# Linear attention and an MLP mixer on one core: the last rows of all eight batches as a ninth batch, part of the normalisation on ScalarE, and a new order of instructions

## The chip, the cores and the metric

One core of a Trainium2 chip runs the whole program. Five engines work side by side, each on its own queue of instructions in program order: TensorE (PE: matrix products into PSUM, eight banks of 128 partitions by 512 fp32 numbers), VectorE (DVE) and ScalarE (ACT), which read PSUM and write SBUF, GpSimd (POOL), and SyncE (SP), which here only issues transfers. An instruction that waits for another engine holds up everything behind it on its own queue. Transfers run on 16 DMA engines. The metric is device time in microseconds (us) of one execution, fp32 in and out, bf16 inside; smaller is better.

## The reference

```python
batch, n_heads, seq, head_dim = (8, 8, 576, 64)     # q, k, v
d_tok, d_ch = (256, 1536)                           # mixer, d_model = 512

def phi(x):
    return np.where(x > 0, x, np.exp(x) - 1.0) + 1.0
q_p, k_p = (phi(q), phi(k))
kv = np.einsum('bhsd,bhse->bhde', k_p, v)
z = np.sum(k_p, axis=2)
num = np.einsum('bhsd,bhde->bhse', q_p, kv)
den = np.einsum('bhsd,bhd->bhs', q_p, z)[..., None] + 1e-06
x = (num / den), heads side by side: (8, 576, 512)

xt = x.transpose(0, 2, 1)
h = np.maximum(xt @ w_tok1, 0.0) @ w_tok2           # along the 576 rows
u = x + h.transpose(0, 2, 1)
h2 = np.maximum(u @ w_ch1, 0.0) @ w_ch2             # along the 512 channels
return (u + h2)
```

The eight batches do not depend on one another. The channel step (`u @ w_ch1`, relu, `@ w_ch2`) works on each row by itself, so rows of several batches can be put together there.

## The kernel before, in words

**Tiling.** The 576 rows of a batch are 64 times 9. Two neighbouring row indices make a tile of 128 partitions: four such row tiles (R = 4, index r) and 64 rows that are left over, the last rows. A batch n goes through these stages:

- loads of q, k, v (`load`, L225, SP's queue), phi of k and q (`phi_exp` on ScalarE, `phi_add` and `phi_end` on VectorE, L250 to L262), the products of k and v (`kv`, L296), a copy to `kvbd` on ScalarE;
- q transposed by transfers on SP (`qtr_dma`, names `nqT0`, `nqT1`, L333), then numerator and denominator (`nd_mm`, name `nn`, 40 products into six banks);
- the division: for batches 2 to 7 `nd_den` and `nd_last` (L395, L404: the sum with eps and the reciprocal, two each, on VectorE) and five multiplications on VectorE, `nd_six` (three times) and `nd_one` (twice);
- the row step (`mm1` L443, `mm2` L454), u = x + h on VectorE (L470), u transposed by transfers on SP (`utr_dma`, L486);
- the channel step. Batches 0 and 1 use plain products there (`mm3` L683, batch 0 also `mm4` L742). From batch 2 on the first product, and from batch 1 on the second, are block products after Strassen and Winograd: seven products of half-size blocks in place of eight, bought with sums and differences of blocks (`u_sums` `nsK`, `row_sums` `nwK`, on VectorE). First product: `mix_mm` (names `nxGI`, group G of three, product I of seven, L913 to L931), read by `mix_read` (`nyGI`: I = 1, 4, 5, 6 on ScalarE, 2, 3, 7 on VectorE). Second product: `product` (`npIJ`, L960 to L972), for batches 1 to 6 read by `pair_copy` (ScalarE), `pair_end` (`neZ` and so on, VectorE) and `pair_more` (`nhZ`, POOL), written out by `pair_put` (`no`, POOL's queue).

**The last rows.** Two batches' last rows fill one tile of 128 rows, `ut`. The pairs (0, 1) and (2, 3) go through the channel step by plain products: `mm3_tail` (names `T00` to `T12`, L706) and `mm4` with t = 8 (`U00` to `U12`). The pairs (4, 5) and (6, 7) come together at the end: `mm3_tails` (`7c0` to `7c5`, L728), then block products (`tail_product`, L1017) with sums on POOL (`tail_sums`), while batch 7 is read in quarters (`product_read`, `product_put`) and its results leave on the queues of SP and ScalarE.

**Order.** `tc.manual_schedule()` is on: the list `ORDER` names every step behind the first batch's start, and each engine executes its own instructions in the order of that list; waits between engines follow from the data. `BANK`, `SLOT`, `EBUF` place each step's PSUM bank and buffer. `A0` to `A43` is the first batch up to its channel step, which the list keeps in the same order in both kernels.

Of the kernel before, what the change touches and what calls it, by code (L numbers as in the profile page):

```python
# [39 lines left out]
WHOLE = {'00', '01', 't0', 't1'}  # L40

BANK = {k_: int(v_) for k_, v_ in (e.split(":") for e in """2K:0 2n0:0 2n1:2 2n2:4 2f:6 2g0:3 2g1:6 2X2:5 2Z2:2 2Y2:1 2gt:6 3K:6 3n0:2 3n1:4 3n2:6 3f:3 3g0:6 3g1:6 3X2:2
3Z2:0 3Y2:5 3gt:4 4K:2 4n0:2 4n1:4 4n2:6 4f:6 4g0:4 4g1:0 4X2:2 4Z2:1 4Y2:3 4gt:6 5K:6 5n0:1 5n1:3 5n2:5 5f:5
5g0:5 5g1:3 5X2:4 5Z2:5 5Y2:7 5gt:1 6K:2 6n0:1 6n1:3 6n2:5 6f:2 6g0:5 6g1:2 6X2:4 6Z2:0 6Y2:6 6gt:6 7K:2 7n0:2
7n1:4 7n2:6 7f:2 7g0:0 7g1:2 7X2:3 7Z2:6 7Y2:1 7gt:5 2m2:0 2m3:1 2m4:2 2m5:3 2m8:1 2m9:1 2m10:0 2m11:1 3m2:0
3m3:1 3m4:2 3m5:3 3m8:1 3m9:0 3m10:0 3m11:1 4m2:0 4m3:1 4m4:2 4m5:3 4m8:1 4m9:1 4m10:0 4m11:1 5m2:0 5m3:1
5m4:2 5m5:3 5m8:1 5m9:0 5m10:0 5m11:1 6m2:0 6m3:1 6m4:2 6m5:3 6m8:1 6m9:1 6m10:0 6m11:1 1h00:7 1h01:6 1h10:5
1h11:6 1t0:7 1t1:0 1t2:1 1t3:6 1m0:2 1m1:0 1m2:0 1m3:4 1m4:5 1m5:6 1m6:6 1m7:2 1m8:5 1m9:7 1m10:1 1m11:6 T00:7
T10:3 T01:3 T11:0 T02:3 T12:7 U08:0 U18:3 7c0:3 7c1:4 7c2:4 7c3:6 7c4:2 7c5:4 7X0:5 7Z0:4 7Y0:1 7X1:2 7Z1:0
7Y1:0 7PX0:7 7PZ0:3 7PY0:1 7PX1:6 7PZ1:5 7PY1:5 7tX:0 7tZ:4 7tY:2 1PX:1 1PZ:2 1PY:5 2PX:0 2PZ:5 2PY:1 3PX:0  # L50
3PZ:3 3PY:4 4PX:7 4PZ:0 4PY:0 5PX:0 5PZ:7 5PY:1 6PX:7 6PZ:1 6PY:6 warm0:0 0Q00:1 0Q01:2 0s0:3 warm1:0 0Q10:1
0Q11:2 warm2:3 0K0:4 0d0:0 0n0:6 0l0:1 0s1:2 0K1:4 0d1:3 0n1:6 0l1:0 0f0:1 0f1:4 0g00:2 0g01:3 0g10:0 0t0:6
0t1:4 0g11:1 0m0:3 0m1:7 0t2:6 0t3:4 0m2:1 0m3:2 0gt:2 0m4:5 0m5:6 0m6:6 0m7:3 0m8:7 0m9:0 0m10:4 0m11:4 U00:1
U01:0 1Q0:4 U02:2 U03:3 1Q1:6 1K:4 1n00:6 1n01:6 1n10:4 1n11:4 1n20:4 1n21:6 1f:4 1g2:4 0ut:3 2X1:6 2Z1:4
2Y1:2 3X1:3 3Z1:5 3Y1:1 4X1:7 4Z1:0 4Y1:0 5X1:6 5Z1:0 5Y1:2 6X1:5 6Z1:6 6Y1:1 2X0:7 2Z0:3 2Y0:0 3X0:4 3Z0:0
3Y0:6 4X0:1 4Z0:7 4Y0:5 5X0:1 5Z0:5 5Y0:0 6X0:7 6Z0:3 6Y0:2""".split())}
# [1141 lines left out]
```

## Time and profile before

| | us |
|---|---|
| runs | 244.52, 245.35, 245.88; median 245.35 |
| span of the profiled execution, first to last instruction | 243.4 |
| PE busy, DVE busy, ACT busy, POOL busy in it | 233.1, 211.5, 136.4, 81.2 |
| end of the last product | 238.5 |
| last product to the end of the span | 4.9 |

The page of the profile shows one execution. Its own span is 243.4 us; what lies around it (start and end of the program) is not in the trace, and the median of the runs lies 1.95 us above it. Busy times are unions of the intervals of an engine's instructions; the shown duration of a matrix product reaches into the next one, so products are costed by the distance of their starts, which the chain of work gives.

### The profile page before, as it was taken

To read this page: it belongs to the slowest core of one execution; us is meant where nothing else is said; L and a number is where in the kernel's file an instruction comes from. 1 tells how busy PE (TensorE), PEld (TensorE's weight loads), DVE (VectorE), ACT (ScalarE), POOL (GpSimd) and SP (SyncE) were. 2 spreads that over 40 slices of the span, in tenths; PEclk is the share of its full clock that TensorE was granted. 3 is DMA by queue.
4 is the path that set the end of the run, shared out by engine and by line. 5 is a ranking of instruction groups with operands and counts; after the bars stand their busy time and mean duration, and the time that the engine had idled before them with its cause. 6 is when DMAs were issued, how large, how long until landed. Compare 5 with 4: busy or idle time off the path is not lost.

```text
span 243.4 us, 6361 instructions
## 1 busy us (share of the span) xinstructions
PE 233.1 (96%) x2597; PEld 174.2 (72%) x2616; DVE 211.5 (87%) x387; ACT 136.4 (56%) x224; POOL 81.2 (33%) x88
## 2 busy tenths in 40 slices
PE   7889989999999999999999999999999999999991
PEld 3575445464677686789867887688778867888881
DVE  5955786999999989999999999999999599867661
ACT  4773782669788277327994297448923542347000
POOL 8870044076910620035200520206015810440730
PEclk9999999999999999999999999999999999999999
DMA  6999989999979989978948989495782285143035
GB/s 230 278 202 260 317 260 234 409 283 286 365 225 198 270 265 161 247 97 305 285 127 175 370 262 200 82 260 178 161 138 40 44 171 112 24 91 81 3 80 180
DMA packets 49805, 48.42 MB, mean 199 GB/s; under 512 B 30064, under 2 KB 35568, under 8 KB 49776
## 3 DMA queue, kind: packets, MB, share of 16 engines
q1 hardware_dynamic: 41664, 35.00, 51.3%
q0 software_dynamic: 7472, 12.22, 25.5%
q10 hardware_dynamic: 640, 0.79, 1.0%
q8 instruction: 20, 0.33, 0.6%
q14 instruction: 9, 0.07, 0.1%
HBM read 35.85 MB, written 9.44 MB: 186 GB/s over the span
## 4 chain that ended last, share of the span: by engine, by line
PE 84%; DMA 9%; POOL 3%; issue 1%; DVE 1%; SPq 1%; POOLq 0%; DVEq 0%
PE ps L970 27%; PE ps L928 23%; PE ps L747 6%; PE ps L448 6%; DMA q_raw<-in_q_dram 5%; PE ps L459 4%; PE ps L686 4%; DMA wc<-in_moe_w_ch_dram 4%; PE ps L711 2%; PE ps L733 2%; PE ps L302 2%; PE ps L1024 2%; PE ps L387 2%; POOL qT L1111 1%; POOL cr L233 1%
## 5 line engine op out<-in xcount | busy, mean ns | idle before, releaser
L970 PE MATMUL ps<-k_raw,v_raw 128*128 128x256 bf16 x252 | 31.8, 273 | 0.0
L943 ACT COPY v_raw<-ps 128x512 f32<-128x512 f32 x30 | 17.0, 595 | 22.7 <-PE ps L928 21.5
L970 PEld LDWEIGHTS <-cr 128*128 128x128 bf16 x252 | 24.4, 98 | 4.8
L970 PEld LDWEIGHTS <-v_raw 128*128 128x128 bf16 x252 | 24.1, 98 | 3.8 <-issue 0.4
L928 PEld LDWEIGHTS <-swc 128*128 128x128 bf16 x240 | 23.4, 98 | 3.1
L681 DVE CUSTOM_DVE_ANT_0 cr<-ps,v_raw 128x512 bf16<-128x512 f32 x30 | 20.1, 684 | 4.5 <-PE ps L928 2.5
L928 PEld LDWEIGHTS <-wc 128*128 128x128 bf16 x216 | 21.1, 98 | 3.6
L928 PE MATMUL ps<-crt,swc 128*128 128x256 bf16 x180 | 23.1, 273 | 0.0
L252 ACT ACTIVATE e<-q_raw 128x1152 bf16<-128x1152 f32 x16 | 18.7, 1167 | 6.7 <-DMA q_raw<-in_q_dram 6.7
L686 PE MATMUL ps<-uT,wc 128*128 128x512 bf16 x91 | 21.6, 379 | 0.4 <-issue 0.2
L970 PE MATMUL ps<-wc,cr 128*128 128x256 bf16 x168 | 21.6, 273 | 0.0
L1071 POOL TENSOR_TENSOR obuf<-obuf,w 128x512 f32<-128x512 f32 x6 | 8.2, 1360 | 38.6 <-ACT w L1058 19.5
L252 ACT ACTIVATE e<-k_raw 128x1152 bf16<-128x1152 f32 x16 | 18.5, 1166 | 3.2 <-DMA k_raw<-in_k_dram 2.6
L1071 POOL TENSOR_TENSOR obuf<-obuf,q_raw 128x512 f32<-128x512 f32 x6 | 8.2, 1374 | 35.6 <-DVE obuf L1064 35.6
L928 PE MATMUL ps<-uT,wc 128*128 128x256 bf16 x144 | 19.5, 273 | 0.0
L1064 DVE TENSOR_TENSOR obuf<-ps,u 128x512 f32<-128x512 f32 x24 | 16.4, 685 | 2.5 <-PE ps L970 2.4
L1071 POOL TENSOR_TENSOR obuf<-obuf,part 128x512 f32<-128x512 f32 x6 | 7.7, 1289 | 26.5 <-DVE dens L400 18.5
L413 DVE TENSOR_TENSOR x<-ps,dens 128x768 bf16<-128x768 f32 x18 | 16.6, 930 | 0.0
L686 PEld LDWEIGHTS <-wc 128*128 128x128 bf16 x96 | 8.9, 98 | 10.0 <-issue 0.6
L470 DVE TENSOR_TENSOR u<-ps,x 128x1024 bf16<-128x1024 f32 x12 | 14.6, 1220 | 0.1
L836 DVE TENSOR_TENSOR v_raw<-cr 128x512 bf16<-128x512 bf16 (+3 forms) x24 | 14.5, 620 | 0.0
L448 PE MATMUL ps<-x,w 128*128 128x512 bf16 x50 | 13.9, 379 | 0.3
(168 smaller groups left out, 514.3 us busy)
## 6 DMA issues: line engine op xcount, KB each, us to landing
k_raw<-in_k_dram SPq DMA_DIRECT2D x16, 576.0 KB, 6.8
q_raw<-in_q_dram SPq DMA_DIRECT2D x16, 576.0 KB, 6.3
v_raw<-in_v_dram SPq DMA_DIRECT2D x14, 576.0 KB, 7.6
out_dram<-obuf POOLq DMA_DIRECT2D x12, 512.0 KB, 6.0
wc<-in_moe_w_ch_dram POOLq DMA_DIRECT2D x8, 384.0 KB, 9.3
out_dram<-obuf POOLq DMA_DIRECT2D x4, 256.0 KB, 7.3
cr<-in_v_dram POOLq DMA_DIRECT2D x2, 288.0 KB, 7.6
out_dram<-obuf POOLq DMA_DIRECT2D x4, 128.0 KB, 4.8
```

The lines of the kernel that those rows point to most:

```text
L252: nc.scalar.activation(out=ebuf[EBUF[f"{n}{nm}{c}"]], in_=f, func=AF.Exp)
L413: nc.vector.tensor_tensor(out=xv[:, :, rc0:rc0 + 3], in0=nd_tile(n, m)[:, :, k0:k0 + 6, 0:D].rearrange("p i (q a) d -> p i q a d", a=2), i ...
L448: nc.tensor.matmul(out=banks(f"{n}f")[:, mt], lhsT=w1t[:, b, ms] if r == R else w1[:, r, ms], rhs=x[b][:, r, :], start=(r == 0), stop=(r = ...
L470: nc.vector.tensor_tensor(out=u[b][:, rs], in0=banks(f"{n}g{i}"), in1=x[b][:, rs], op=ALU.add)
L681: nc.vector._custom_dve(TENSOR_ADD_SAT, out=o, in0=ps, in1=c, s0=3.4028234663852886e38, s1=0.0)
L686: nc.tensor.matmul(out=bank(f"{n}m{mc}"), lhsT=wc1[:, kj, 128 * mc:128 * mc + 128], rhs=uTj[b][:, kj] if n < 2 - U1 else uT[b][:, :, kj], ...
L747: nc.tensor.matmul(out=bank(f"U{p}{t}"), lhsT=crt[:, kc, :] if t == 8 else cr[b][:, kc, 128 * r:128 * r + 128], rhs=wc2[:, kc, :], start=( ...
L928: nc.tensor.matmul(out=ps[:, j], lhsT=lhs[:, k_, 128 * j:128 * (j + 1)], rhs=rhs[:, :, k_], start=(first and j == 0 and k_ == 0), stop=(k_ ...
L943: nc.scalar.copy(out={1: c1, 6: c6, 5: c5}[i], in_=ps)
L970: nc.tensor.matmul(out=ps, lhsT=lhs[:, k_], rhs=rhs[:, k_], start=(first and not skip and k_ == 0), stop=(k_ == KH - 1), skip_group_check= ...
L1064: nc.vector.tensor_tensor(out=slots(f"{n}P", 4)[:, d::2, HC[c]], in0=pair_tile(n, "X" if z == "W" else z), in1=u[n % 2][:, d::2, HC[c]], o ...
L1071: nc.gpsimd.tensor_tensor(out=o, in0=o, in1=part[i], op=ALU.add)
```

## The change

The last rows of all eight batches become a ninth batch (n = 8) with four row tiles, one for each pair of batches: `ut` is now 128 by 4 by 512, `uTt` holds its transpose, and `mix_mm`, `mix_read`, `row_sums`, `product` now run up to n = 8, and `product_read` for n = 8 alone. Batch 7 is treated like batches 1 to 6; batch 8 takes the place that batch 7 had, without its own table of weight sums. `mm3_tail`, `mm3_tails`, `tail_product` and what belongs to them are gone. The last rows of x have a tile of their own (`xt`), in which a batch writes only its 64 partitions, and the sum u of a pair is one instruction of 128 partitions (`mm2_tails_read`, `ngv`) in place of two of 64.

In the division, the sum with eps goes to ScalarE in three pieces (`nd`: names `nd0` to `nd2`), one reciprocal covers all 42 denominators (name `nnd`), the two multiplications of 128 elements become four scaled copies on ScalarE (`no0`, `no1`), and the third large one is split in two (`nn2`, `nnt`). `BANK`, `SLOT`, `EBUF` and the list `ORDER` behind `A43` are new as a whole; in the new list the two halves of a bank (`p10 p11`) follow one another.

```diff
-NO = 6
+NO = 4
...
-CUTS = {1: [0, 3, 6], 2: [0, 2, 6], 3: [0, 2, 6], 4: [0, 2, 6], 5: [0, 2, 6], 6: [0, 2, 6], 7: [0, 2, 4, 6]}
+CUTS = {1: [0, 3, 6], 2: [0, 2, 6], 3: [0, 2, 6], 4: [0, 2, 6], 5: [0, 2, 6], 6: [0, 2, 6], 7: [0, 2, 6], 8: [0, 2, 4, 6]}
...
-WHOLE = {'00', '01', 't0', 't1'}
+WHOLE = {'00', '01'}
...
-0mb1 0mb0 0ma6 0r0 0mb3 0r1 1ka0 0ma7 1kx0 0ma2 0ma8 0mb6 1kb0 0mb2 0r3 0mb8 0mb7 0r6 0r8 0ma4 0r7 G21 0gt
-1kx1 G22 0ma9 0gv 0ma10 0mb4 1ka1 0r2 0ma5 0r4 G11 0mb10 1kb1 0mb5 0r10 G23 0mb9 0r5 0ma11 0mb11 1qa0 1qx0 B0
-0r9 0q0 B1 0r11 1qb0 B2 1qx1 1qa1 1Q00 1Q01 0q1 1Qc01 1v0 1Qc00 0q2 1qb1 1v1 1Q10 1Q11 1K 1Qc11 2Lq0 ws02
-1Qc10 0q3 2Lq1 1Kc0 1Kc1 2Lv0 ws04 1n20 1n01 2Lk0 1nc20 0q4 2Lk1 1nc01 2Lv1 1n10 0q5 1nc10 1n00 0q6 1nc00 1n11
...
-6kx1 3p21 3w20 4uT1 5qb1 3p10 5Kc1 6kx0 3w22 3p11 5qT1 3eZ 3p50 3c0 6ka1 3p51 5Kc0 5qT0 3w40 U10 3c2 3w30 U11
-6Lq0 6Lq1 6kb1 U12 4s1 6ka0 3p31 V1 3p30 7Lk0 4s2 6Lv1 3p61 3eY 6Lv0 3p60 6kb0 7Lk1 5n 3c1 5nd 3hY 3p71 5ne
-3p70 5n0 3hZ 4x02 5o0 3eW 4x01 4x21 5n2 4y01 3hW 3p40 4y21 4y02 4x06 6qx0 5n1 4x05 4x26 4y06 6qa1 3p41 4y05
...
-7ta1 7R11 7R51 7p20 7w32 7t5 7R10 7ts2 7R50 7p61 7tb1 7p31 7R61 7ts4 7R20 7p30 7R31 7tr5 7p60 7tr1 7ts3 7p71
-7R60 7p21 7t6 7R21 7R30 7p70 7R71 7D200 7tr6 7t3 7D711 7D710 7ta2 7D201 7tr3 7D210 7R70 7tb2 7p41 7D311 7tr2
-7D310 7t7 7D211 7R41 7td20 7p40 7D411 7tr7 7D410 7t4 7td21 7R40 7D700 7D701 7tr4 7td70 7td71"""
...
+A31 A32 A35 A34 A36 A37 A38 1Lk0 A39 1Lk1 1Lv1 A40 1Lq0 A41 1Lq1 A42 1Lv0 A43 0ma0 At2 0ma1 At3 0ma3 0mb1 0ma5 G03
+0ma4 G01 1kx0 1ka0 1kb0 B0 G02 0ma7 0r1 G21 0mb4 0mb7 G22 0mb3 0r4 B1 0r3 0r7 0ma6 0mb6 1kx1 G11 0mb0 0r0 0mb5 G23
+0ma8 0ma2 0r6 1ka1 1kb1 0r5 0mb2 0r2 1v1 B2 2Lq0 2Lq1 0ma11 0mb11 0ma9 0mb9 G24 G13 G04 0r11 0ma10 0mb10 2Lv0 2Lk0 0r9
+1qx0 0r10 0q1 1qa0 1qb0 1qa1 1qx1 1qb1 0q0 1Q00 1Qc00 0mb8 0r8 1Q01 1Qc01 1v0 0q2 2Lk1 G12 1Q10 1K 1Qc10 G14 1Q11
+1Qc11 0q3 1Kc1 1Kc0 1n01 2qx0 2Lv1 1n00 wt0 ws04 ws14 1nc01 0q4 0q5 1n20 0q6 1nc00 1n21 0q7 1nc20 ws24 ws02 1nc21 1n10
...
+3y15 5v1 3y17 5K 5Kc0 3x04 5Kc1 3x13 3x24 3x14 3y04 4g1 3y14 6Lk1 5qb1 3p10 4gu0 3y13 3p11 5qT0 3y24 3p20 6qx0 3w10
+3w12 3p21 4gu1 3w22 3c0 3w20 3p50 3p51 3c2 3p61 3eZ 5qT1 5n 6kx1 3p60 6ka1 3w40 3p30 3w30 5d0 5d2 5d1 5nd 3p31 3c1 5o1
+6kb1 5n0 4uT0 5o0 3eY 3p71 6kx0 3p70 3eW 4x01 4x02 4uT1 4s1 5n2 3hZ 6qx1 4x12 5nt 3p40 7Lk1 3p41 4y01 4y02 4x11 4y11
+4x21 4y21 3eX 3hY 6Lv1 6v1 7Lv1 4s2 5n1 4x05 4x22 4y22 4x16 4x06 4y06 5f0 6qa1 7Lq1 3hW 3o 4y05 4s3 5f1 4x26 4x07 4y12
...
+8s3 7x24 8x15 8y16 8x21 8y06 8x05 7y24 7y17 7x14 8s4 8y21 8y05 8x07 7y14 8x26 8y07 8x17 8x03 7y22 7p10 7w20 7w12 8x02
+8y03 8x12 7p11 8y15 8y17 7c0 8y12 7p50 8y26 8x13 8y02 7w22 7w40 8x04 8x25 8y04 8y25 8x22 8y22 8x27 7w30 6o 7p20 7p21
+7eZ 7p61 7p60 8y27 7c1 8x23 8w10 8y23 7p51 7hZ 8y13 8x14 8x24 8y24 8w34 8w32 8w14 7p71 7p70 7eW 8w20 8w40 8p10 8y14
+7c2 8w12 8w30 8R10 7p30 7p31 7eY 7p40 7p41 8p51 7eX 8p11 8R11 8p21 7hW 8R21 8D210 8p20 7hY 8w24 8w22 8R51 8p50 8R50
+8D211 8w42 8w44 8p61 8R61 8p60 8R60 8R20 8p30 8R30 8D200 8D201 8p31 8p70 8p71 8R70 8p40 8R31 8D311 8D310 8R71 8p41
+8D710 8D711 8R40 8D701 8D700 8R41 8D411 7o 8D410"""
...
-    x = [const(f"x{b}", [128, R1, DM]) for b in range(2)]
+    x = [const(f"x{b}", [128, R, DM]) for b in range(2)]
+    xt = [const(f"xt{i}", [128, DM]) for i in range(2)]
-    ut = [const(f"ut{i}", [128, DM]) for i in range(2)]
+    ut = const("ut", [128, R, DM])
-    uTt = const("uTt", [128, 2, NDM, 128])
+    uTt = const("uTt", [128, R, NDM, 128])
...
+    dens = work.tile([128, 3, 2, 7], FP32, name="dens", tag="dens", bufs=1)
+    eps = work.tile([128, 1], FP32, name="eps", tag="eps", bufs=1)
...
-    def nd_den(n):
-        at = BANK[f"{n}n0"]
-        assert BANK[f"{n}n1"] == at + 2
-        nd_tile(n, 0), nd_tile(n, 1)
-        both = psum[:, at:at + 4, 0:D1 * 7].rearrange("p b (k e) -> p b k e", k=7)
-        nc.vector.tensor_scalar(out=dens.rearrange("p m i k -> p (m i) k"), in0=both[:, :, :, D],
-                                scalar1=EPS, scalar2=None, op0=ALU.add)
-        nc.vector.reciprocal(out=dens, in_=dens)
-
-    def nd_last(n):
-        nc.vector.tensor_scalar(out=last, in0=nd_tile(n, 2)[:, :, 0:6, D], scalar1=EPS,
-                                scalar2=None, op0=ALU.add)
-        nc.vector.reciprocal(out=last, in_=last)
+    def nd_den(n, m):
+        w = 7 if m < 2 else 6
+        nc.scalar.activation(out=dens[:, m, :, 0:w], in_=nd_tile(n, m)[:, :, 0:w, D],
+                             func=AF.Identity, bias=eps)
+
+    def nd_inv():
+        d = dens.rearrange("p m i k -> p (m i k)")
+        nc.vector.reciprocal(out=d, in_=d)
+
+    def nd_scale(o, n, m, k0, k1, h=slice(0, 128)):
+        q_ = (k1 - k0) // 2
+        nc.vector.tensor_tensor(
+            out=o, in0=nd_tile(n, m)[h, :, k0:k1, 0:D].rearrange("p i (q a) d -> p i q a d", a=2),
+            in1=dens[h, m, :, k0:k1].rearrange("p i (q a) -> p i q a", a=2)[
+                :, :, :, :, None].to_broadcast([h.stop - h.start, 2, q_, 2, D]), op=ALU.mult)
 
     def nd_six(n, m):
-        k0, rc0 = (m, 4 * m) if m < 2 else (0, 7)
         xv = x[n % 2].rearrange("p r (c i a d) -> p i (r c) a d", c=2, i=2, a=2)
-        den = (dens[:, m] if m < 2 else last)[:, :, k0:k0 + 6]
-        nc.vector.tensor_tensor(
-            out=xv[:, :, rc0:rc0 + 3],
-            in0=nd_tile(n, m)[:, :, k0:k0 + 6, 0:D].rearrange("p i (q a) d -> p i q a d", a=2),
-            in1=den.rearrange("p i (q a) -> p i q a", a=2)[
-                :, :, :, :, None].to_broadcast([128, 2, 3, 2, D]), op=ALU.mult)
+        if m < 2:
+            nd_scale(xv[:, :, 4 * m:4 * m + 3], n, m, m, m + 6)
+        else:
+            nd_scale(xv[:, :, 7:8], n, 2, 0, 2)
+
+    def nd_tail(n):
+        h = half[n % 2]
+        xv = xt[n // 2 % 2].rearrange("p (c i a d) -> p i c a d", c=2, i=2, a=2)
+        nd_scale(xv[h], n, 2, 2, 6, h)
 
     def nd_one(n, m):
         at = (6, 0)[m]
         xv = x[n % 2].rearrange("p r (c i a d) -> p i (r c) a d", c=2, i=2, a=2)
-        nc.vector.tensor_tensor(
-            out=xv[:, :, 3, m], in0=nd_tile(n, m)[:, :, at, 0:D],
-            in1=dens[:, m, :, at, None].to_broadcast([128, 2, D]), op=ALU.mult)
+        for i in range(2):
+            nc.scalar.activation(out=xv[:, i, 3, m], in_=nd_tile(n, m)[:, i, at, 0:D], func=AF.Copy,
+                                 scale=dens[:, m, i, at:at + 1])
 
     for n in range(2 - U1, B):
         put(f"{n}n", nd_mm, n)
-        put(f"{n}nd", nd_den, n)
-        put(f"{n}ne", nd_last, n)
+        for m in range(3):
+            put(f"{n}d{m}", nd_den, n, m)
+        put(f"{n}nd", nd_inv)
         for m in range(3):
             put(f"{n}n{m}", nd_six, n, m)
+        put(f"{n}nt", nd_tail, n)
...
-    def mm2_tails_read(p, b):
-        h = half[b]
-        nc.vector.tensor_tensor(out=ut[p % 2][h], in0=bank(f"{2 * p + 1}gt")[h], in1=x[b][h, R],
-                                op=ALU.add)
+    def mm2_tails_read(p):
+        nc.vector.tensor_tensor(out=ut[:, p], in0=bank(f"{2 * p + 1}gt"), in1=xt[p % 2], op=ALU.add)
...
-    def mm3_tail(p, i):
-        ps = bank(f"T{p}{i}").rearrange("p (m s) -> p m s", m=4)
-        for m in range(4):
-            mc = 4 * i + m
-            for kj in range(NDM):
-                nc.tensor.matmul(out=ps[:, m], lhsT=wc1[:, kj, 128 * mc:128 * mc + 128],
-                                 rhs=uTt[:, p, kj, :], start=(kj == 0), stop=(kj == NDM - 1))
...
-    def mm3_tails(i):
-        ps = bank(f"7c{i}").rearrange("p (h e s) -> p h e s", h=2, e=2)
-        for h in range(2):
-            mc = NCH // 2 * h + i
-            for kj in range(NDM):
-                nc.tensor.matmul(out=ps[:, h], lhsT=wc1[:, kj, 128 * mc:128 * mc + 128],
-                                 rhs=uTt[:, :, kj, :], start=(kj == 0), stop=(kj == NDM - 1))
...
+    sb8 = [raw["k", 0].rearrange("p j f -> p (j f)").bitcast(BF16)[:, 1536 * i:1536 * (i + 1)]
+           for i in range(3)] + [raw["q", 0].rearrange("p j f -> p (j f)").bitcast(BF16)[:, 0:1536]]
+    sb8 = [t.rearrange("p (k j s) -> p k j s", k=KH, j=2) for t in sb8]
...
-        if n == B - 1:
-            s_, t, c0 = sw, tu, 256 * g
-        else:
-            s_, t, c0 = [swc[:, GSW[g], w] for w in range(4)], tuc, 0
+        s_, t = [swc[:, GSW[g], w] for w in range(4)], tuc
         w_ = lambda m, h: cblock(m, h)[:, :, 256 * g:]
-        lhs, rhs = {1: (w_(0, 0), ublock(0, 0, b)), 2: (w_(0, 1), ublock(1, 0, b)),
-                    3: (s_[3][:, :, c0:], ublock(1, 1, b)), 4: (w_(1, 1), t[3]),
-                    5: (s_[0][:, :, c0:], t[0]), 6: (s_[1][:, :, c0:], t[1]),
-                    7: (s_[2][:, :, c0:], t[2])}[i]
+        lhs, rhs = {1: (w_(0, 0), ublock(n, 0, 0)), 2: (w_(0, 1), ublock(n, 1, 0)),
+                    3: (s_[3], ublock(n, 1, 1)), 4: (w_(1, 1), t[3]), 5: (s_[0], t[0]),
+                    6: (s_[1], t[1]), 7: (s_[2], t[2])}[i]
         for j in range(2):
...
+    out8 = [t.rearrange("p c t i d -> p (c t i d)").bitcast(FP32)[:, 0:2 * DM].rearrange(
+        "p (r d) -> p r d", r=2) for t in (kp, qp)]
+    for n in range(1, B + 1):
...
-    def tail_sums(which):
-        after(winograd(ts, ta, which, slice(0, KH), nc.gpsimd),
-              live["row", B - 1, 4, 4] if which == 1 else None)
...
-    for n in range(1, B - 1):
+    for n in range(1, B):
...
+    nc.vector.memset(eps, EPS)
+    nc.vector.memset(dens, 1.0)
+    for t in xt:
+        nc.vector.memset(t, 0.0)
```

## The prediction

> **What bounds the kernel now.** I read the page first, then the chain that ended last, then busy times by stretches, then the groups of instructions by shape.
>
> ```profile
> span 243.4 us, 6361 instructions
> PE 233.1 (96%) x2597; PEld 174.2 (72%) x2616; DVE 211.5 (87%) x387; ACT 136.4 (56%) x224; POOL 81.2 (33%) x88
> ...
> PEclk9999999999999999999999999999999999999999
> ```
>
> TensorE is busy for nearly the whole span, at a granted clock of nine tenths or more in every slice. The stretches (length, busy time of PE, weight loads, DVE, ACT, POOL, then clock, DMA share, GB/s) show who else is full:
>
> ```profile
> 23.00:44.60 21.60, 20.66 (x188) 10.27 (x189) 16.06 (x37) 12.02 (x18) 5.89 (x6) 1.00 1.06 285
> 44.60:127.50 82.90, 82.16 (x1024) 60.08 (x1033) 80.63 (x141) 58.90 (x89) 27.21 (x25) 1.00 0.93 248
> 127.50:174.90 47.40, 47.19 (x527) 37.62 (x533) 46.34 (x83) 30.30 (x49) 10.88 (x11) 1.00 0.80 216
> 174.90:238.60 63.70, 63.51 (x651) 53.62 (x652) 52.27 (x100) 22.15 (x43) 22.00 (x21) 1.00 0.40 82
> ```
>
> From 44.6 to 174.9 VectorE idles 3.3 of 130.3 us and TensorE 1.0: two engines are full at once. Behind 174.9 VectorE has 11.4 us free and TensorE none. The chain gives the distance of products (start, length, piece):
>
> ```profile
> 63.72 0.89 PE ps L711 x16
> ...
> 98.27 3.27 PE ps L970 x30
> ...
> 222.12 2.62 PE ps L733 x24
> ...
> 237.84 0.69 PE ps L1024 x6
> 238.55 0.42 DVE obuf L1031
> ```
>
> So a product of 128 columns takes 0.0556 us, one of 256 columns 0.109; four of 512 columns (0.86 in the same view, L747) 0.2155 each. From 44.6 on the chain is TensorE alone, to 238.5; then one VectorE read and a transfer, 4.9 us to the end of the span. The groups of the division (busy, mean ns):
>
> ```profile
> L413 DVE TENSOR_TENSOR x<-ps,dens 128x768 bf16<-128x768 f32 x18 | 16.6, 930 | 0.0
> L483 DVE TENSOR_TENSOR ut<-ps,x 64x512 bf16<-64x512 f32 x6 | 4.1, 687 | 0.1
> L422 DVE TENSOR_TENSOR x<-ps,dens 128x128 bf16<-128x128 f32 x12 | 3.2, 281 | 0.0
> L402 DVE RECIPROCAL dens<-dens 128x28 f32<-128x28 f32 x6 | 2.0, 328 | 0.2
> L407 DVE RECIPROCAL dens<-dens 128x12 f32<-128x12 f32 x6 | 1.4, 228 | 0.2
> L619 ACT ACTIVATE x<-ps,den 128x64 bf16<-128x64 f32 x8 | 1.8, 324 | 0.0
> ```
>
> **TensorE.** Removed: T00 to T12, 96 products of 128 columns, 5.34; U00 to U12, 24 of 512, 5.17; 7c0 to 7c5, 48 of 256, 5.24; the seven tail products, 42 of 256, 4.59; 0gt and 1g2, four of 512, 0.86; 0ut, four transposes (0.22 as in L538's pieces). Sum 21.42. Added: 84 mix products and 84 block products of 256 columns, 168 x 0.1092 = 18.35, and 1gt, four of 64 rows (0.55, as L478). Sum 18.90. **Net -2.52 us**, all on the bound. It is uneven: 11.0 us leave among batches 1 to 6, and 8.5 come to the end (18.35 - 5.24 - 4.59).
>
> **VectorE.** The division of a batch: now 0.181 + 0.328 + 0.135 + 0.228 (two sums, two reciprocals) + 3 x 0.930 + 2 x 0.281 = 4.22. After: a reciprocal of 42 (0.228 at 12 and 0.328 at 28 extend to 0.416), 2 x 0.930, a 256-wide piece (0.424, L364's shape), a 64x512 piece (0.687, L483's shape): 3.39. Six batches: -5.0. Last rows: eight reads of 64 partitions (5.5) become four of 128 by 512 (0.687 each): -2.75; V0, V1 -1.37; seven tail reads -2.94; the weight sums 7F2 to 7F4 -2.85; batch 7's row sums in fewer pieces -0.9. Added: nine mix reads 6.17, four differences 1.75, twelve row sums 5.0, batch 7's four pair reads 2.74. Sum -0.1: the same work, but 9.1 of it moves out of the full stretch into the one with 11.4 free. The start's four more memsets (two like kvbd's 0.275, two tiny) stand before a wait of 1.12 for the first k: hidden.
>
> **ScalarE.** Removed T and 7c reads 6.8, 0uc 0.6. Added twelve mix reads 7.2, batch 7's three copies 1.8, 24 scaled copies of 64 columns at 0.324 (L619, the same form) 7.8, and 18 sums with eps. No row shows these; the nearest are 0.161 (64x2 cast, L567) and 0.324: 2.9 to 5.8, I take 4.5, nearer the form with a pointer operand. +13.9 on an engine with 89.2 of 130.3 busy in the full stretch: hidden except where an instruction behind it is awaited. The trace's only table load took 1.283 for Exp, Relu and Copy together; Identity is new. If it needed another table, twelve switches would cost ScalarE 15.4; I take none. The Trainium skill ("ScalarE: Activation LUTs", "Table sets: the hidden batching unit") lists copy, relu and identity as fillers of every set, which the single load bears out for the first two; no run here shows Identity. Its section "Rules for kernel authors" speaks against this part: adds and multiplications belong on VectorE. By rows that is 4.5 + 7.8 = 12.3 on ScalarE for 5.0 off VectorE, a bad trade by itself; with VectorE full and ScalarE at 68% in the stretch it stands here, and the rule is one reason for the third rival.
>
> **Queues.** POOL loses tail_sums 6.8, first_sum 4.2 and four issues 2.7, gains three adds (1.34 each) and two issues (0.63): off the path. B0 to B2 move up, past no other POOL instruction, and 2q0's load still waits for wc2's second piece, so the loads start no sooner (37.9). SP gains one transpose (1ut, 1.25 to issue). In the new order 5qT stands before 4uT on SP; 4u's last sum stands 6.0 us of products ahead of 4x01, the two issues of 5qT take 2.9 and 4u's landing 3.1: the room is used up, cost 0 to 0.5, I take 0.
>
> **The end.** 7o, two transfers of 512 KB on POOL's queue, is new there. Thirteen product steps of 0.655 follow 7p41, so 7eX ends some 7.6 before the last product; issues 1.3 and landing 6.0 (the median of such transfers) end at about -0.3. Together with batch 8's 1 MB the last 11 us carry 2 MB, 180 GB/s, which the last slice of the page (180) shows as possible. Last read, last 64 KB transfer: as before. 0, bounds -0.3 to +1.
>
> **Given back.** What the sum hangs on is VectorE's lead. Adding row means over the order: before, the entries up to 5qb1 are 108.2 us of VectorE work, done in 96.7 busy us by 127.5 (factor 0.89), with 7.8 idle; 5n starts at 135.6, 7.4 after the end of 5qb1, which q's two transposing transfers (2.9 to issue, 4.7 to land) use up. After: 98.9 x 0.89 = 88.4, 8.3 less; TensorE's entries before 5n fall from 111.3 to 98.3, 13.0 less. So VectorE may idle only 7.8 - 4.7 = 3.1 before TensorE waits at 5n. Its named idle stretches: 1.08 for k (now G03, G01, 0.7, stand before it), 1.22 for an exp that stood behind two reads (now ahead of them, about 0.4), 0.91 for q (0r9 and three G now ahead), 0.77 for transposes (1v0, G12), 1.11 for the first denominators (wt0, 0.95): 5.1 become some 1.0. Of the other 2.7, 1.1 is waiting for products, which a later VectorE does not do: 1.6. New: the reciprocal waits for ScalarE (three sums, and an exp of 1.17 if one is running, less VectorE's own work between: 0 to 2.5 over batches 2 to 4), I take 1.0. Sum 3.6 against 3.1: **+0.5**; bounds 0 and, with the idle time of before, 4.7.
>
> **Sum.** 243.4 - 2.52 + 0.5 = 241.4 of span. The median of the runs lies 1.95 above the span: **243.3 us**, -0.8%.
>
> **Rivals.**
> - *Nothing is given back, and TensorE's own idle time before 44.6 (0.94) goes too.* For: all five idle stretches have work in front now. Against: the new order leaves less lead everywhere. 245.35 - 2.52 = 242.8, down to 241.9.
> - *Slower: VectorE loses its lead.* Place: the wait of 5n (and 1K, 1t, 2f before it) for VectorE. If it idles 7.8 as before, 4.7 is given back: 245.35 - 2.52 + 4.7 = 247.5; with all of the reciprocals' 2.5, 250.0. It decides from 5.6 us of idle time before 5qb1. For: rows of a full VectorE; a lead cut by more than half. Against: the waits of before were for other causes, which the list treats.
> - *ScalarE becomes the late one.* With the sums above it is 82% full in the stretch (97 of 119), and one exp holds it 1.17. If two of the six batches expose one exp each at a bank that TensorE needs: +2.3, 245.35 - 2.52 + 2.3 = 245.1. For: its waits of before were already up to 1.6 for kvbd; against: most were long waits for products (21.5 at L943).
>
> **How the numbers follow.** The likeliest has 0.43 (its own range 242.6 to 244.1), nothing given back 0.20, the lost lead 0.21, ScalarE 0.16. A difference under 0.5% (244.1 to 246.6) can hardly be told from none. Faster: 0.43 + 0.20, less 0.01 for its edge; slower: 0.21 less its small cases, 0.18; same: 0.16 and what is left of the others, 0.20. The range reaches from 241.6 (first rival, with the end's -0.3) to 247.0, into the lost lead: 0.05 below, 0.13 above.
>
> **What would show it.** Right: the last product ends near 236.5; some 168 more products at 0.109; VectorE's idle time up to 5qb1 near 3.6; TensorE's waits behind 44.6 within 1 us; TensorE to end 4.9. Wrong: TensorE waiting 2 us or more at L387, L302 or L448 for VectorE; `dens` reciprocals waiting for ScalarE by over 0.5 each; a second table load; span minus last product above 6.

## The result and the profile after

The changed kernel takes 259.17 us (median of 4 runs, 257.99 to 260.58), the kernel before on the same chip 245.62 us. The ratio is 1.0567 with a 95% interval of 1.0521 to 1.0613: slower, and outside the range that was forecast. The page of the changed kernel (the span; busy times of PE, weight loads, DVE, ACT and POOL; then TensorE's busy tenths and its granted clock in 40 slices of 6.4 us):

```profile
span 256.2 us, 6331 instructions
PE 236.2 (92%) x2570; PEld 174.8 (68%) x2570; DVE 225.8 (88%) x374; ACT 147.7 (58%) x268; POOL 78.4 (31%) x79
...
PE   7899999959699999998999999799999999999991
...
PEclk9999999979999999999999999999999999999997
```

The span grew by 12.8 us, and VectorE's busy time by 14.3 (from 211.5), where the prediction had its work unchanged. TensorE's busy time grew too, with fewer products, and the ninth slice, in which TensorE is half idle, shows a lower clock. By stretches (columns as in the prediction; the last line is the stretch in which the clock, third from the end, was low):

```profile
23.00:44.60 21.60, 20.85 (x190) 10.58 (x189) 19.35 (x42) 11.69 (x18) 5.07 (x5) 1.00 1.05 285
44.60:127.50 82.90, 75.38 (x906) 52.22 (x904) 79.98 (x115) 59.12 (x102) 28.40 (x25) 0.98 0.91 255
127.50:174.90 47.40, 44.96 (x503) 35.55 (x501) 45.06 (x70) 31.24 (x58) 12.95 (x10) 1.00 0.81 181
174.90:238.60 63.70, 63.70 (x656) 53.76 (x654) 54.44 (x90) 32.80 (x63) 12.99 (x11) 1.00 0.43 79
54.80:58.20 3.40, 3.40 (x17) 1.58 (x17) 3.37 (x7) 1.80 (x3) 0.00 (x0) 0.50 1.34 198
```

Between 44.6 and 174.9 TensorE now idles 10.0 us (7.5 + 2.4, rounded apart), against 1.0 before, and 1409 products are recorded there instead of 1551. VectorE is nearly as full as before. Behind 174.9 nothing is lost. TensorE's two longest waits between 44.6 and 174.9 (us in all, times, longest) are for VectorE:

```profile
PE ps L530 <- DVE obuf L681: 2.4, 1, 2.4
PE ps L871 <- DVE q_raw L753: 1.6, 1, 1.6
```

So VectorE is busy and TensorE waits for it; the question is with what VectorE is busy. Its groups by shape (out<-in, count, then busy time, mean ns, idle time in front):

```profile
L258 DVE TENSOR_TENSOR qp<-e,y 128x1152 bf16<-128x1152 bf16 x16 | 15.5, 971 | 0.6 <-ACT e L248 0.2
L252 DVE TENSOR_SCALAR y<-q_raw 128x1152 bf16<-128x1152 f32 x16 | 14.1, 884 | 0.3
L734 DVE TENSOR_TENSOR k_raw<-wc 128x1536 bf16<-128x1536 bf16 x2 | 5.0, 2498 | 0.0
L399 DVE RECIPROCAL dens<-dens 128x42 f32<-128x42 f32 x6 | 2.5, 412 | 0.5 <-ACT dens L394 0.5
```

The first three shapes and counts are in the kernel before too, with means of 749, 775 and 951 ns. The same instructions take 1.3, 1.14 and 2.6 times as long. The new reciprocal costs what was estimated (0.416), and it waits 0.5 us for ScalarE in all six batches together.

What holds them is seen in the timeline (start, length, instruction). VectorE of the changed kernel:

```profile
46.64 1.52 DVE L258 TENSOR_TENSOR qp<-e,y 128x1152 bf16<-128x1152 bf16 x1
48.20 1.60 DVE L252 TENSOR_SCALAR y<-q_raw 128x1152 bf16<-128x1152 f32 x1
49.91 1.53 DVE L258 TENSOR_TENSOR qp<-e,y 128x1152 bf16<-128x1152 bf16 x1
...
53.00 0.68 DVE L681 TENSOR_TENSOR obuf<-ps,u 128x512 f32<-128x512 f32 x1
```

and GpSimd in the same stretch, where `weight_sums` runs (differences of blocks of the second channel weights, 12 instructions of 128x512, 1.16 alone):

```profile
45.88 1.67 POOL L726 TENSOR_TENSOR q_raw<-wc 128x512 f32<-128x512 bf16 x1
47.63 1.56 POOL L726 TENSOR_TENSOR k_raw<-wc,q_raw 128x512 bf16<-128x512 bf16 x1
49.26 3.19 POOL L726 TENSOR_TENSOR q_raw<-wc,q_raw 128x512 f32<-128x512 bf16 x2
```

Where both engines have such instructions one behind the other, they run in strict turns: VectorE's take 1.52 to 1.60 instead of 0.75, GpSimd's 1.56 to 1.67 instead of 1.16, and one of each starts about every 1.6 us. The read of PSUM behind them (L681) has its 0.68. Run 7 below has the same 374 VectorE instructions in the same order, without GpSimd's differences and additions. Set beside it, 18 of the changed kernel's VectorE instructions take over 60 ns longer, all of them beside a GpSimd difference or addition, 14.5 us together; the two of L734 are 3.1 of that. VectorE's busy time is 13.6 us longer than in run 7 (225.8 against 212.2).

The kernel before had the same work on both engines and did not lose by it:

```profile
59.41 0.75 DVE L262 TENSOR_TENSOR kp<-e,y 128x1152 bf16<-128x1152 bf16 x1
60.19 0.76 DVE L256 TENSOR_SCALAR y<-q_raw 128x1152 bf16<-128x1152 f32 x1
60.87 1.28 DVE L693 TENSOR_SCALAR cr<-ps 128x512 bf16<-128x512 f32 x2
62.07 0.75 DVE L262 TENSOR_TENSOR qp<-e,y 128x1152 bf16<-128x1152 bf16 x1
```

```profile
60.31 7.41 POOL L816 TENSOR_TENSOR q_raw<-wc,q_raw 128x512 f32<-128x512 bf16 x5 [1.57 <-DVE kp L262]
```

There GpSimd pays: of the five differences three take 1.56 to 1.79 us and two 1.16, while of VectorE's instructions beside them only one is longer, by 0.08 (at 67.50). VectorE's SBUF instructions lie apart there, with reads of PSUM between them. Of the three that hold a difference up, those at 60.19 and 65.95 began before it; the one at 62.07 is recorded 0.02 behind it. What arranged this is a wait written by hand in `weight_sums`, which the change leaves as it is:

```
first = {(0, 0): ("phi", "q", 2, 1), (2, 0): ("phi", "k", 2, 1)}.get((i, k0))
after(nc.gpsimd.tensor_tensor(...), live[first] if first else None)
```

In the order before, `ws00` and `ws20` head two groups of the differences on GpSimd's queue (`ws02 ws04 ws14`, `ws00 ws10 ws24 ws12`, `ws20 ws30 ws34 ws22 ws32`), so that the two waits hold both groups until phi of batch 2 is done. In the new order the queue reads `ws04 ws14 ws24 ws02 ws12 ws22 ws32 ws00 ws34 ws10 ws20 ws30`: both waits stand late and hold back nothing that matters. Seven differences run before and beside phi of batch 2, and the other five from 61.1 on, four of them beside phi of batch 3 (1.71 at 64.03, 1.60 at 65.78, 1.75 at 68.50).

The Trainium skill ("SBUF — State Buffer", section "Who interferes with whom") describes this: VectorE and GpSimd share a pair of SBUF ports; VectorE needs it in its faster modes and when both its inputs are in SBUF, and whichever engine starts first holds it for a whole instruction while the other stands still. The traces agree, with the numbers above. L681 has one input in SBUF and one in PSUM, and its 0.68 agrees with the Trainium skill's exception for instructions with at most one SBUF input outside the faster modes.

### The profile page after: what moved, and what is told of

It reads as the page before. It is cut to its first block, busy times and chain, and to the rows that moved or that the text cites. A ratio compares the mean times of both kernels' runs of the same rounds, so it can differ in the third digit from the quotient of the medians.

```text
span 256.2 us, 6331 instructions
## 1 busy us (share of the span) xinstructions
PE 236.2 (92%) x2570; PEld 174.8 (68%) x2570; DVE 225.8 (88%) x374; ACT 147.7 (58%) x268; POOL 78.4 (31%) x79
## 4 chain that ended last, share of the span: by engine, by line
PE 47%; DVE 23%; DMA 16%; issue 6%; POOL 3%; ACT 2%; SPq 0%; DVEq 0%; POOLq 0%
PE ps L829 21%; PE ps L871 15%; PE ps L451 5%; DMA uT<-u 5%; DMA qT<-qp 4%; DMA k_raw<-in_k_dram 4%; DMA wc<-in_moe_w_ch_dram 4%; PE ps L463 4%; DVE y L252 3%; DVE qp L258 3%; DVE x L403 2%; DVE obuf L918 2%; DVE kp L258 2%; DVE cr L649 1%; DVE k_raw L753 1%
## 5 line engine op out<-in xcount | busy, mean ns | idle before, releaser
L925 POOL TENSOR_TENSOR obuf<-obuf,q_raw 128x512 f32<-128x512 f32 x7 | 13.3, 1903 | 82.0 <-DVE obuf L918 68.4
L829 PEld LDWEIGHTS <-swc 128*128 128x128 bf16 x336 | 32.8, 98 | 7.8 <-DVE sums L791 1.4
L829 PE MATMUL ps<-sums,swc 128*128 128x256 bf16 x252 | 33.2, 273 | 1.5 <-DVE sums L791 1.1
L871 PEld LDWEIGHTS <-cr 128*128 128x128 bf16 x288 | 28.0, 98 | 5.4 <-issue 0.8
L829 PEld LDWEIGHTS <-wc 128*128 128x128 bf16 x252 | 24.5, 98 | 5.9 <-issue 1.8
L649 DVE CUSTOM_DVE_ANT_0 cr<-ps,v_raw 128x512 bf16<-128x512 f32 x35 | 23.2, 683 | 5.3 <-ACT w L844 2.6
L844 ACT COPY v_raw<-ps 128x512 f32<-128x512 f32 x35 | 19.9, 593 | 9.5 <-PE ps L829 8.9
L925 POOL TENSOR_TENSOR obuf<-obuf,part 128x512 f32<-128x512 f32 x7 | 9.2, 1310 | 26.3 <-ACT dens L394 15.5
L654 PEld LDWEIGHTS <-wc 128*128 128x128 bf16 x96 | 9.3, 100 | 11.6 <-issue 2.7
L842 ACT ACTIVATE cr<-ps 128x512 bf16<-128x512 f32 x21 | 12.0, 598 | 8.4 <-PE ps L829 5.9
L258 DVE TENSOR_TENSOR qp<-e,y 128x1152 bf16<-128x1152 bf16 x16 | 15.5, 971 | 0.6 <-ACT e L248 0.2
L469 DVE TENSOR_TENSOR u<-ps,x 128x1024 bf16<-128x1024 f32 x12 | 14.5, 1217 | 0.0
L252 DVE TENSOR_SCALAR y<-q_raw 128x1152 bf16<-128x1152 f32 x16 | 14.1, 884 | 0.3
## 6 DMA issues: line engine op xcount, KB each, us to landing
out_dram<-obuf POOLq DMA_DIRECT2D x4, 256.0 KB, 7.5
```

The costliest lines, as they stand in the source:

```text
L252: nc.vector.tensor_scalar(out=ybuf[YBUF[f"{n}{nm}{c}"]], in0=f, scalar1=1.0, scalar2=1.0, op0=ALU.add, op1=ALU.max)
L258: live["phi", nm, n, c] = nc.vector.tensor_tensor(out=dst.transpose([0, 2, 1, 3]), in0=e.rearrange("p (i t d) -> p i t d", i=2, t=T), in1= ...
L469: nc.vector.tensor_tensor(out=u[b][:, rs], in0=banks(f"{n}g{i}"), in1=x[b][:, rs], op=ALU.add)
L649: nc.vector._custom_dve(TENSOR_ADD_SAT, out=o, in0=ps, in1=c, s0=3.4028234663852886e38, s1=0.0)
L654: nc.tensor.matmul(out=bank(f"{n}m{mc}"), lhsT=wc1[:, kj, 128 * mc:128 * mc + 128], rhs=uTj[b][:, kj] if n < 2 - U1 else uT[b][:, :, kj], ...
L829: nc.tensor.matmul(out=ps[:, j], lhsT=lhs[:, k_, 128 * j:128 * (j + 1)], rhs=rhs[:, :, k_], start=(first and j == 0 and k_ == 0), stop=(k_ ...
```

## Experiments

Theories: **P**, that VectorE and GpSimd hold each other up, as at a shared port; **O**, the redrawn order by itself; **N**, the denominators' way over ScalarE; and, from the second group of runs on, **D**, the transfers around the transposes, and **V**, VectorE's own work. Ratios are to the kernel before on the same chip.

**1. Without the differences.** `a_no_ws`:

```diff
-ws04 ws14 ... ws30                      (all twelve out of ORDER)
-            6: (s_(1), tb[1], False)
+            6: (s_(1), wblock(1, 1), False)
-            4: (a_(1, 1), tb[3], False)
+            4: (a_(1, 1), wblock(1, 0), False)
```

> The changed kernel with GpSimd's twelve weight differences left out; two of the four difference blocks are replaced by plain blocks of the weights in the products, so TensorE's work keeps its shape and batches 1 to 8 are computed with wrong weights. Theory P (the differences run beside VectorE's instructions that read and write SBUF, and the two hold each other up: 13.5 us of VectorE's time): nearly all of the loss goes, 244 to 249 us, VectorE's sum falls from 225.8 to 211 to 214, no phi product over 0.80 us between 45 and 72 us. Theory O (the redrawn order itself, with transposes that land late around 100, 110 and 130 us): little changes, 255 to 260 us. Theory N (the denominators' way over ScalarE) gives 255 to 260 as well.

Measured 251.55 us, ratio 1.0261 (1.0236 to 1.0286): 7.6 us of the loss, about half. VectorE's sum fell to 216.3, not to 211 to 214; no phi instruction between 45 and 72 us takes over 0.80. Its stretches 44.6 to 127.5 and 127.5 to 174.9:

```profile
44.60:127.50 82.90, 79.17 (x953) 56.57 (x959) 78.83 (x123) 62.49 (x108) 14.98 (x15) 1.00 1.01 270
127.50:174.90 47.40, 44.86 (x498) 35.80 (x502) 44.68 (x72) 31.07 (x59) 9.56 (x9) 1.00 0.82 181
```

TensorE still idles 6.3 us, and now VectorE is not full either. P holds for the first half of the loss; the rest needs another cause.

**2. The same in the kernel before.** `b_no_ws`, the same edit there:

> The kernel before without its twelve differences, the same replacement in the products. Their collisions in its trace cost VectorE 1.0 us in all and GpSimd's own waits cost nothing: 244 to 245.5 us, so that the changed kernel without differences still stands 6 to 7 us behind its counterpart. If the differences cost the kernel before as much as the changed one: 237 to 239 us.

Measured 245.15 us, ratio 1.0008 (0.9983 to 1.0033). The differences cost the kernel before nothing: the 7.6 us come from where the new order puts them.

**3. The kernel before with its waits taken away.** `b_ws_free`:

```diff
-        first = {(0, 0): ("phi", "q", 2, 1), (2, 0): ("phi", "k", 2, 1)}.get((i, k0))
+        first = None
```

> The kernel before with the two waits taken away that held its last nine differences behind phi of batch 2; nothing else is changed. Theory P: the differences then run at once behind the third, from 43 us on, beside phi of batch 2, and the kernel before loses 2 to 6 us (247.5 to 251.5 us), with phi's instructions over 1.3 us in that stretch. Theories O and N: 245 to 246 us, as before.

Measured 253.5 us, ratio 1.0343 (1.0305 to 1.0381): 8.2 us, more than the 2 to 6 expected, and most of it in another place. The first seven came early and lengthened two VectorE instructions by 1.9 us. Then VectorE, a little later than before, came with its own SBUF instructions in a row upon GpSimd's issues of output transfers (57.04 to 60.00) and, from 60.02 on, the last five differences:

```profile
58.66 1.72 DVE L262 TENSOR_TENSOR kp<-e,y 128x1152 bf16<-128x1152 bf16 x1
60.42 1.60 DVE L256 TENSOR_SCALAR y<-k_raw 128x1152 bf16<-128x1152 f32 x1
61.94 1.91 DVE L824 TENSOR_TENSOR k_raw<-wc 128x1536 bf16<-128x1536 bf16 x1
```

In the kernel before these take 0.75, 0.76 and 0.95. The first of them had run for 1.36 us before a difference began; it was held beside the issues (see the last section). VectorE's busy time rises by 6.6 us and the span by 7.8. Two waits that look like mere order are worth 8 us in a kernel that is otherwise untouched; of all the runs this one shows P most plainly.

**4. The differences placed by hand.** `a_ws_placed`:

```diff
+ORDER: ws02 ws04 ws14 early; ws00 ws10 ws24 ws12 behind 2qb1; ws20 ws30 ws34 ws22 ws32 behind 3qb0
-(2, 0): ("phi", "k", 2, 1)
+(2, 0): ("phi", "q", 3, 0)
```

> The changed kernel with the twelve differences in the groups of the kernel before: three early, four that wait for phi of batch 2's second q half, five that wait for phi of batch 3's first q half (so that they fall beside reads of PSUM). Theory P: 246 to 251 us, the collisions of 46 to 53 and 63 to 70 us gone, some of the last five still meet phi of batch 3's k. Theories O and N: 255 to 260 us.

Measured 263.71 us, ratio 1.0757 (1.0704 to 1.0809), a miss by 13 us. Up to 63 us the mend works (the end of phi of batch 3's first q half comes at 63.2 instead of 70.2). But the two output transfers of batch 0 are issued from GpSimd's queue too, and now stood behind the last group; it kept meeting VectorE's instructions (one difference took 5.19 us), so the outputs left at 74 us instead of 60, and VectorE stood still for the buffer:

```profile
DVE obuf L917 <- DMA out_dram<-obuf: 9.0, 1, 9.0
```

**5. The same, with the last group behind the output transfers.** `a_ws_late` (the five behind `0o0` in ORDER, otherwise as 4):

> The changed kernel with the differences in three groups (three early, four behind phi of batch 2's second q half, five behind phi of batch 3's first q half), and the last five now stand behind both output transfers of batch 0 on GpSimd's queue, so that no output waits for them. Theory P (collisions on the SBUF port): within 2 us of the kernel without any differences, 250 to 254 us. If collisions were not what the removal of the differences had bought, but only their absence from GpSimd's queue or the weights' earlier readiness, it stays at 257 to 260 us.

Measured 254.28 us, ratio 1.0375 (1.0348 to 1.0401), with the whole computation: 4.9 of the 7.6 us come back from moving twelve instructions of an engine that is a third busy. The rest stays: a phi instruction of batch 2 still takes 1.38 at 55.1, and the last five differences take 10.7 us (64.3 to 75.0), so that a copy of ScalarE's whose target overlays their operand (`pair_copy`, L911) waits 2.0 for them and TensorE 1.7 for the copy.

**6. The differences on VectorE.** `a_ws_vector`:

```diff
-        after(nc.gpsimd.tensor_tensor(out=o[:, ks], in0=x_[:, ks], in1=y_[:, ks],
+        after(nc.vector.tensor_tensor(out=o[:, ks], in0=x_[:, ks], in1=y_[:, ks],
```

> The changed kernel with the twelve differences on VectorE, at the same places of the order. They are 128x512 with one fp32 side, 0.4 to 0.7 us each alone, so 5 to 8 us more work on the engine that bounds the stretch. Theory P: 13.5 us of holding go and 5 to 8 come, 250 to 255 us. Theories O and N: the work is simply added, 262 to 268 us.

Measured 261.17 to 265.78 us in four runs, ratio 1.0727 (1.063 to 1.0824): outside P's 250 to 255 us, and by the ratio, 263.1, inside the 262 to 268 of O and N. It does not decide between them, because the move cost more than the work. The differences take 0.68 each, 8.2 us, but VectorE also waited 3.5 us at one of them for the weights to arrive, where GpSimd had waited beside it, and late ones held weight loads of products up by 3.3.

**7. Without GpSimd's additions as well.** `a_no_pool` (`pair_more`, L925: 21 additions of 128x512 fp32 that complete the block products of batches 1 to 7; all `h` entries out of ORDER, on top of 1):

> The changed kernel without the differences and without the 21 additions of GpSimd that complete batches 1 to 7 (parts of the outputs are missing); GpSimd then only issues transfers. Theory P for these additions too: VectorE's u_sums, row sums and phi that they hold up lose 3.7 us of excess in the sum, of which only the first two or three lie where VectorE is the limit: 1 to 2.5 us under the kernel without differences, 249 to 250.5 us. If they cost nothing: 251 to 252 us.

Measured 247.6 us, ratio 1.01 (1.0071 to 1.0129): 3.9 us under run 1, more than expected. No VectorE instruction is now slowed by more than 0.2 us beside GpSimd, and VectorE's sum is 212.2. In run 1 the slowed ones were few, but among them are `u_sums` (0.42 become 1.15), whose result the next block products wait for.

**8. The same in the kernel before.** `b_no_pool`:

> The kernel before without its twelve differences and without its 18 additions on GpSimd (parts of the outputs are missing). If GpSimd costs the kernel before nothing anywhere: 244 to 246 us, and the 12 us that the changed kernel gains from the same removal are the new order's own. If the additions hold VectorE up here too: 241 to 243.5 us.

Measured 246.13 us, ratio 1.003 (1.0008 to 1.0053). GpSimd's additions are free in the old order as well. So all 11.6 us of 1 and 7 are the new order's own.

**9. Fewer bytes of input.** `a_light_loads`, on top of 1:

```diff
+        w = slice(0, TD // 2 if n >= 4 else TD)
-        ... dma_start(out=raw[nm, rb(n)][:, js], in_=src_[:, js]) ...
+        ... dma_start(out=raw[nm, rb(n)][:, js, w], in_=src_[:, js, w]) ...
```

> The changed kernel without the differences, and the loads of batches 4 to 7 fetch the first half of each row alone (half of what phi reads is old data). Theory D (what is left of the loss, TensorE idle for about 5 us between 95 and 175 us, is transposes that land 6 to 8 us after their issue because the inputs of later batches go over the same DMA engines): transposes land in 3 to 5 us, the waits for qT, uT and their sums shrink by 3 us or more, 246 to 249 us. Theory V (VectorE's own work in that stretch): 250 to 252 us, unchanged.

Measured 248.07 us, ratio 1.012 (1.0087 to 1.0153): 3.5 us under run 1, as D has it. The median from issue to landing of q's transposes falls from 7.1 to 5.3 us, not quite to the 3 to 5 expected.

**10. All three at once.** `a_quiet` (7 and 9 together):

> The changed kernel with all three suspects taken away at once: no differences and no additions on GpSimd, and the loads of batches 4 to 7 fetch half of each row (outputs wrong in batches 1 to 8). If the port (P) and the transfers in front of the transposes (D) are all that was lost, the plan is left: TensorE idles under 1.5 us between 44.6 and 175 us, span 242 to 244, 243.5 to 245.5 us, just under the kernel before. If something else stands in the order, TensorE still idles 3 us or more there: 246 to 248 us.

Measured 243.64 us, ratio 0.9923 (0.9894 to 0.9951), a span of 242.0. Stretches of run 7, then of this run:

```profile
44.60:127.50 82.90, 80.53 (x1002) 57.55 (x1001) 78.76 (x126) 62.85 (x111) 4.99 (x8) 1.00 1.00 275
127.50:174.90 47.40, 46.09 (x537) 36.75 (x537) 44.67 (x74) 31.66 (x56) 2.61 (x4) 1.00 0.81 178
```

```profile
44.60:127.50 82.90, 82.33 (x1020) 60.20 (x1026) 81.14 (x129) 64.45 (x117) 5.01 (x8) 1.00 0.82 222
127.50:174.90 47.40, 47.24 (x589) 37.97 (x591) 45.82 (x74) 32.93 (x60) 2.63 (x4) 1.00 0.63 133
```

TensorE's idle time goes from 3.7 to 0.7 us, and the time comes within 0.4 us of the predicted 243.3. Taken away in this order, the three costs add up to the loss: 259.2, less 7.6 (differences), 3.9 (additions) and 4.0 (load bytes). But this run does less work than the kernel before that it is compared with. Without GpSimd's two groups that kernel gained nothing (run 8); with fewer input bytes it was not run, but its TensorE idles only 1.0 us in these two stretches.

**11. Loads behind the transposes.** D leaves two readings: the loads stand in the wrong places of SyncE's queue, or there is too much to move in the time. `a_loads`, on top of 5, moved seven loads; in it one of them (v of batch 5, first half) came behind the cast that reads it, which then took old data, other than its expectation says.

```diff
+ORDER: 5Lq0 5Lv1 behind 4qT1; 5Lv0 5Lk1 behind 3uT1; 6Lq1 6Lk1 behind 5qT1; 7Lq1 behind 6qT0
```

> The changed kernel with the differences in three groups and, on SyncE's queue, seven loads moved behind the transposes that they stood in front of (two halves of batch 5 behind q of batch 4, two behind u of batch 3, two of batch 6 behind q of batch 5, one of batch 7 behind q of batch 6). The same computation, nothing left out. Theory D: q's transposes land in 4 to 5 us, TensorE idles 2 us less, 251 to 253 us. If the loads are then late themselves, phi waits for them and it stays at 254 to 256 us.

Measured 257.69 us, ratio 1.0485 (1.0445 to 1.0526), 3.4 us worse than run 5. One phi of batch 6 waited 4.3 us for its k, which had been moved to just ahead of it.

**12. Four of these loads, on the kernel without collisions.** `a_no_pool_loads`, on top of 7, with the four that have 30 or more entries of ORDER between their new place and their use:

```diff
+ORDER: 5Lq0 5Lv1 behind 4qT1; 6Lq1 behind 5qT1; 7Lq1 behind 6qT0
```

> The changed kernel without GpSimd's differences and additions (as before, parts of the outputs are missing), full loads, and four loads moved behind the transposes that they stood in front of (two of batch 5 behind q of batch 4, one of batch 6 behind q of batch 5, one of batch 7 behind q of batch 6). It stood at 247.6 us without the move and at 243.6 us with half of the loads' bytes taken away. If the places in the queue are the cost: q's transposes land in 4.5 to 5.5 us and 245 to 246.5 us. If it is the bytes as such, with the loads needed just as soon as the transposes: 247 to 249 us, with waits of phi for k or q in place of those for qT.

Measured 248.69 us (247.22 to 250.48), ratio 1.0109 (1.0074 to 1.0144), against 247.6 in run 7: nothing gained. From issue to landing (min, median, max), q's transposes in the kernel before, after, in run 7, in run 10 and in this run:

```profile
DMA to landing us min/median/max: 3.6/4.7/6.7
...
DMA to landing us min/median/max: 3.6/6.3/8.5
...
DMA to landing us min/median/max: 4.5/6.9/8.5
...
DMA to landing us min/median/max: 3.6/4.9/8.5
...
DMA to landing us min/median/max: 3.5/5.7/8.6
```

q's transposes gain 1.2 us by the move, but the u transposes lose: their median goes from 3.6 to 5.3, and `u_sums` waits 5.5 us for them instead of 4.4. For these four loads it is the bytes, then, and not the places; as the four runs lie 3.3 us apart, a small gain cannot be ruled out. That a load of half the size also reaches phi sooner is part of run 9's gain and was not told apart.

**13. The denominators back on VectorE.** `a_den_vector`:

```diff
-        nc.scalar.activation(out=dens[:, m, :, 0:w], in_=..., func=AF.Identity, bias=eps)
+        nc.vector.tensor_scalar(out=dens[:, m, :, 0:w], in0=..., scalar1=EPS, scalar2=None, op0=ALU.add)
```

> The changed kernel with the 18 sums with eps back on VectorE (reads of PSUM, about 0.15 each by the 0.181 and 0.135 of the profile before), nothing else changed. Theory N (the reciprocal's way over ScalarE costs): 255 to 258 us. By the traces, where the reciprocals wait 0.5 us in all: VectorE has 2.7 us more work, about two thirds of it in the full stretch, 259 to 262 us.

Measured 262.11 us, ratio 1.0655 (1.0596 to 1.0714), about 3 us slower than the changed kernel by the medians, though the intervals of the two ratios just overlap. N falls: taking that part of the change back does not help, and it is worth some 2 to 3 us.

**14. All mends together.** `a_mended`: run 5, the four moves of run 12, and three additions held behind the difference they ran into:

```diff
+        behind = {(1, "W"): ("us", 2, 2), (3, "Y"): ("us", 4, 2), (4, "Y"): ("us", 5, 4)}.get((n, z))
+        after(nc.gpsimd.tensor_tensor(out=o, in0=o, in1=part[i], op=ALU.add),
+              live[behind] if behind else None)
```

> The whole computation: the changed kernel with the differences in three groups behind phi, the same four loads moved, and three of GpSimd's additions held until the difference of VectorE's that they ran into is done (batch 1's W, batch 3's Y, batch 4's Y). The removals were worth 7.6 (differences), 4.0 (additions) and 4.0 us (loads); placing the differences kept 4.9 of the 7.6. With half of the other two: 250 to 252 us. If additions and loads only change what they collide with: 253 to 256 us. Under 245 us only if all three came back whole.

Measured 255.46 us (253.37 to 256.0), ratio 1.0388 (1.0355 to 1.0422), no better than run 5. Two of the three run free; the third meets the next `u_sums` instead (1.50 at 138.4). Another addition, which none of the waits touch, now runs into a `u_sums` too (1.48 at 106.8), and q's and u's transposes wait as in run 12. With these means no version of the whole computation beat the kernel before; what the change could give, with all three costs away, is run 10's 0.8%.

## Why the prediction was wrong

The forecast was 243.3 us, the time 259.2, with 0.18 for slower. Two steps failed. Run 10, from which what they overlooked is taken away, has a span of 242.0 against the forecast 241.4, so the rest of the sum nearly stands.

- **Queues, "off the path" for POOL.** This is the step that failed worst: 11.6 of the 15.9 us, where the sum has nothing. The prediction listed what GpSimd loses and gains and looked for work that waits for it. It did not ask beside which VectorE instructions GpSimd's remaining entries come to lie. Both ORDER lists and the hand-written wait were at hand; the trace before shows the price only on the side that did not count (differences of GpSimd's at 1.56 to 1.79 instead of 1.16).
- **Given back, the busy half of it.** VectorE's idle time before the end of `5qb1` was forecast to fall by 4.2 us. Adding up VectorE's instructions in the traces, it fell by 3.3, from 14.1 to 10.8, counted from its first instruction on. But its busy time up to there, forecast to shrink by 8.3, grew from 113.2 to 115.5; without GpSimd's two groups (run 7) it is 106.1, 7.1 less. The work sum used row means of an execution without collisions.
- **Given back, "4.7 to land".** The landing of q's transposes was taken over from the old order. It became 6.3, and 6.9 once the collisions were gone and phi came sooner. The change takes 11 us of TensorE's work out of the batches' stretch and leaves the input bytes in it; the DMA share of 44.6 to 127.5 rose from 0.93 to 1.00 in run 7. The sum has no term for that; run 10 puts it at about 4.0 us.
- **TensorE, -2.52.** Right as work. By the shapes that run 7 and run 2 (before) record, there are 78 more products of 256 columns, 26 fewer of 512, 100 fewer of 128 and 2 more of the short kind with 64 columns of weights: 46 fewer in all, as forecast; at the prediction's distances that is -2.4 us. The busy times show only -1.3 (233.3 us in 2616 products, 232.0 in 2570), but a product that TensorE pauses behind counts in them with its whole shown duration (0.273 for 256 columns, at a distance of 0.109), and run 7 idles 3.7 us in the two stretches where run 2 idles 0.1. The changed kernel itself has the same 2570 products in 236.2. Of these 4.2 us more, some 1.7 are the clock (an estimate: 3.4 us at half of it): it was 0.50 from 54.8 to 58.2, just behind TensorE's longest wait (2.4 us, to 53.7). The Trainium skill ("TensorE: Matmul & The Clock Gate", Part 1) says that a TensorE left idle gets a slower clock until it has been busy again; this stretch agrees.
- **VectorE, -0.1.** Right as work: 212.2 in run 7 against 212.5 in run 8. The reciprocal (0.412 for 0.416) and the scaled pieces (0.945, 0.409, 0.682 for 0.930, 0.424, 0.687) were right.
- **ScalarE, +13.9 hidden.** +11.3 (147.7 against 136.4), the sums 0.27 each, the scaled copies 0.312; one table load, as assumed. Hidden, by run 13 a gain. The rival of a late ScalarE did not come.
- **The end, 0.** The last product ends at 250.5, 5.7 before the end of the span, against 4.9: within the bounds, +0.8.
- **The rivals.** "VectorE loses its lead" has the right place, TensorE waiting for VectorE (the longest wait, L530, is `1t`, which it names), but its condition (5.6 us of idle time before `5qb1`) did not decide, and its 247.5 to 250.0 is too low. A VectorE that is late by being busy longer was not among the cases, so the range had no room for it.

Of the 7.6 us of the differences the clock has some 1.7 at most, going by the two profiled executions: run 1's clock is full up to its last product. Open: whether another order could hold the new plan with full loads.
